# The begin of a kernel: 20 products of zeros, first loads in three pieces, token rows ahead of w1, statistics and the centring of w1 reordered

## The chip, the cores and the metric

The kernel runs on one core of a Trainium2 chip. The metric is device time in microseconds (us). Before the change the median of three runs is 933.14 us (932.35 to 933.66). One more execution was recorded by the hardware profiler; it took 934.63 us, and every start time below counts from the first instruction of that record.

A core has five engines that run side by side, each through its own list of instructions in order, and wait for each other by semaphores: TensorE (PE: matrix products, with its weight loads shown as PEld), VectorE (DVE), ScalarE (ACT), GpSimd (POOL) and SyncE (SP, which here only issues transfers). Transfers are issued by SP and ACT and carried by 16 shared DMA engines.

## The reference, cut to what matters

For S = 2048 tokens of D = 448 channels the kernel computes two branches of the same input x and mixes them by a gate:

```python
g = sigmoid((x * gate_w).sum(-1, keepdims=True))
a = attention(x, wq, wk, wv, wo)        # 16 heads of 28, one shared k and v
h = gelu(layernorm(x) @ w1)
hs = shifted(h) @ w2                    # four channel groups shifted by +1, -1, +2, -2 tokens
x1 = x + hs
b = x1 + gelu(layernorm(x1) @ w3) @ w4
return g * a + (1 - g) * b
```

The change is in the front part: the projection x @ wq (q, with k, v and the gate packed into spare columns) and the preparation of layernorm(x) @ w1.

## The kernel before, in words

**Number format.** Products that must be accurate are done as three products of split operands. A raw 32-bit tile is copied into a rounded "high" tile (`ah`, `wqh`, `w1h`; ACT) and the rest is kept in a "low" tile (`al`, `wql`, `w1l`; DVE). High by high, high by low and low by high are then summed in PSUM (`proj`, L132 to L139). The functions `split_x`, `split_w_chunk`, `split_w_high` and `split_w_low` do the splitting.

**Tiles.** xT holds x transposed, channels on partitions, in four chunks (c = 0 to 3) of 128 channels, the last one half full and held twice. Tokens are taken in four blocks b of 512. wq is laid out in the same four chunks; its 512 columns are four groups g of 128.

**Order.** The order of each engine's instructions is the order in which they stand in the program; nothing is rescheduled. Eight completion counters for transfers are handed round in program order, so that a transfer waits until the earlier transfer with its counter has landed.

**The front part, in order.**
- DVE clears `warm`, and PE multiplies it by itself 16 times (L97), products of zeros into `warm_ps` that nobody reads.
- ACT issues four transfers, one for each chunk of wq (L284), and SP four, one for each chunk of x of block 0 (L285), 256 KB each. Then ACT loads its table for Gelu (L286).
- `load_x(1)` brings x of block 1 (1 MB), then w1 (0.9 MB, L474). `load_x(2)` reuses the buffer of `wqraw`, and so waits for the last split of wq. Behind it come the token rows of blocks 0 and 1 (`load_x1`, 0.9 MB each, tile `x1`), w2 and the token rows of block 2.
- `first_queries` makes q of block 0 for the four groups. Chunk 0 is taken in full 32-bit products straight from the raw tiles (L316), since it has landed before anything is split; one such instruction is done as two passes, so that four instructions show as eight records. Chunks 1 to 3 follow as split products (L320).
- `stage_q(u)` for u = 4 to 11 makes q of blocks 1 and 2, 11 products each; ACT copies the result into one of four `qf` buffers (L308) and issues its write to memory (L309).
- For the layer norm before w1, only the factor 1/sqrt(var + eps) is applied after the product: `ln1_tile(b, t)` takes mean and variance of 128 tokens (DVE, L143 and L144; after the fourth, POOL raises to the power -0.5, L147 and L148), `ln1_send(b)` transposes the four columns on PE into the one-bank PSUM tile "misc" (L369), has ACT copy them (L371) and SP write them out, `ln1_read(b)` reads them back on every partition (`rsb`). The mean is taken off the weights instead: `sum_w1` adds the chunks of w1 on POOL (L385 to L387), `centre_w1` adds over partitions by a product with ones on PE, also into "misc" (L391), and takes the mean off each column on DVE (L393). `split_w_high` and `split_w_low` then split the centred w1.
- `stage_w1(0)` is the first stage that reads w1 (products `h`, L135 to L139); its results are scaled by `rsb` (L445).

In the program before, `sum_w1` stands behind the copies of `first_queries`, the statistics of block 0 behind `stage_q(5)`, `centre_w1` behind `stage_q(6)`, the sending of the statistics behind `stage_q(8)`, and the statistics of block 1 between `split_w_high` and `split_w_low`. The rest of the kernel (w2, w3 and w4, then attention with its exponentials) is not touched.

Of the kernel before, what the change touches and what calls it, by code (L numbers as in the profile page):

```python
# [10 lines left out]
F32R = mybir.dt.float32r  # L11
AF = mybir.ActivationFunctionType
# [4 lines left out]
P = 128  # L17
S = 2048
D = 448
# [17 lines left out]
def f32(ap):  # L37
    return ap.bitcast(F32)
# [3 lines left out]
def gated_mix_kernel(  # L42
# [12 lines left out]
    nc = tc.nc  # L55
# [18 lines left out]
    first = keep.tile([P, 4], F32, name="first")  # L74
    epst = keep.tile([P, 4], F32, name="epst")
    powt = keep.tile([P, 4], F32, name="powt")
# [12 lines left out]
    def misc_tile(name):  # L89
        return psA.tile([P, 512], F32, tag="misc", bufs=1, name=name)  # L90
# [2 lines left out]
        return psA.tile([P, 512], F32, tag="mx", bufs=1, name=name)  # L93

    wps = misc_tile("warm_ps")
    for _ in range(16):
        nc.tensor.matmul(wps[:, 0:256], warm[:, 0:P], warm, start=True, stop=True)  # L97

    def split_w_chunk(raw, wh, wl, c, cols=slice(None)):
# [9 lines left out]
    def split_w_high(raw, wh, wl):  # L109
        nc.scalar.copy(wh[:, 0:3, :], raw[:, 0:3, :])  # L110
        nc.gpsimd.memset(f32(wh)[64:128, 3, :], 0.0)
        nc.scalar.copy(wh[0:64, 3, :], raw[0:64, 3, :])
        nc.scalar.copy(wl[64:128, 3, :], raw[64:128, 3, :])

    def split_w_low(raw, wh, wl):
        for c in range(3):
            nc.vector.tensor_tensor(wl[:, c, :], raw[:, c, :], f32(wh)[:, c, :], ALU.subtract)
        nc.vector.tensor_tensor(wl[0:64, 3, :], raw[0:64, 3, :], f32(wh)[0:64, 3, :], ALU.subtract)
# [22 lines left out]
    def stats_tile(pool, b, t, mv):  # L141
        st = pool.tile([P, 6], F32, tag="st", bufs=4, name=f"st_{pool.name}_{b}_{t}")
        nc.vector.bn_stats(st, x1[:, 4 * b + t, :])  # L143
        nc.vector.bn_aggr(mv[:, t, :], st)  # L144

    def stats_end(mv, rs):
        nc.gpsimd.tensor_tensor(rs, mv[:, :, 1], epst, ALU.add)  # L147
        nc.gpsimd.tensor_tensor(rs, rs, powt, ALU.pow)  # L148

    def stats_tiles(pool, b):  # L150
        return (pool.tile([P, 4, 2], F32, tag="mv", bufs=2, name=f"mv_{pool.name}_{b}"),
                pool.tile([P, 4], F32, tag="rs", bufs=2, name=f"rs_{pool.name}_{b}"))
# [99 lines left out]
    with tc.tile_pool(name="s1b", bufs=1) as s1b, \  # L252
# [13 lines left out]
        xraw, xact = {}, {}  # L266

        def load_x(b):
            if b == 1:
                xraw[b] = f32(s1b.tile([P, 4, 512], F32R, tag="w2x", bufs=1, name="xkv_1"))  # L270
            else:
                xraw[b] = s1.tile([P, 4, 512], F32, tag="raw", bufs=2, name=f"xkv_{b}")
            nc.sync.dma_start(xraw[b], xT[:, :, 512 * b:512 * b + 512])

        def load_x1(b):
            nc.sync.dma_start(x1[:, 4 * b:4 * b + 4, :],
                              x[512 * b:512 * b + 512, :].rearrange("(t p) d -> p t d", p=P))

        wqraw = s1.tile([P, 4, 512], F32, tag="raw", bufs=2, name="wqraw")
        wqh = s1.tile([P, 4, 512], F32R, name="wqh")  # L280
        wql = s1.tile([P, 4, 512], F32R, name="wql")
        xraw[0] = s1.tile([P, 4, 512], F32, tag="raw", bufs=2, name="xkv_0")
        for c in range(4):
            nc.scalar.dma_start(wqraw[:, c, :], wq[:, c, :])  # L284
            nc.sync.dma_start(xraw[0][:, c, :], xT[:, c, 0:512])  # L285
        nc.scalar.activation(first, powt, AF.Gelu_apprx_tanh)  # L286
        w1h = s1.tile([P, 4, D], F32R, name="w1h")
        w1l = s1.tile([P, 4, D], F32R, name="w1l")
        w2h = s1b.tile([P, 4, D], F32R, name="w2h")
        w2l = s1b.tile([P, 4, D], F32R, name="w2l")  # L290
        hh, hl, acts = {}, {}, {}

        def split_x(b, c0, c1, high=True):
            if b not in xact:
                xact[b] = (s1.tile([P, 4, 512], F32R, tag="ah", bufs=3, name=f"ahk_{b}"),
                           s1.tile([P, 3, 512], F32R, tag="al", bufs=3, name=f"alk_{b}"))
            split_a(xraw[b], *xact[b], c0, c1, high)
# [7 lines left out]
        def q_out(u, ps):  # L305
            b, g = divmod(u, NG)
            qf = s1.tile([P, 512], F32, tag="qf", bufs=4, name=f"qf_{u}")
            nc.scalar.copy(qf, ps)  # L308
            nc.scalar.dma_start(qd[g, :, 512 * b:512 * b + 512], qf)  # L309
# [13 lines left out]
        def stage_q(u, tile_of=mm1):  # L323
            b, g = divmod(u, NG)
            ps = tile_of(f"q_{u}")
            w = slice(g * P, (g + 1) * P)
            proj(ps, wqh[:, :, w], wql[:, :, w], *xact[b])
            q_out(u, ps)
# [31 lines left out]
        def ln1_tile(b, t):  # L360
            if t == 0:
                rs1_of[b] = stats_tiles(s1, b)
            stats_tile(s1, b, t, rs1_of[b][0])
            if t == 3:
                stats_end(*rs1_of[b])

        def ln1_send(b):
            ps = misc_tile(f"rsT_{b}")[0:4, 0:P]
            nc.tensor.transpose(ps, rs1_of.pop(b)[1], ident)  # L369
            rT = s1.tile([4, P], F32, tag="rT", bufs=2, name=f"rT_{b}")  # L370
            nc.scalar.copy(rT, ps)  # L371
            rb_of[b] = dram.tile([4, P], F32, tag="rsd", bufs=2, name=f"rsd_{b}")
            nc.sync.dma_start(rb_of[b], rT)

        def ln1_read(b):
            rd = rb_of[b]
            rb_of[b] = s1.tile([P, 512], F32, tag="rsb", bufs=2, name=f"rsb_{b}")
            nc.sync.dma_start(rb_of[b][0:C], rd.rearrange("(o t) p -> o (t p)", o=1).broadcast_to([C, 512]))
# [5 lines left out]
        def sum_w1():  # L384
            nc.gpsimd.tensor_tensor(wsum, w1raw[:, 0, :], w1raw[:, 1, :], ALU.add)  # L385
            nc.gpsimd.tensor_tensor(wsum, wsum, w1raw[:, 2, :], ALU.add)
            nc.gpsimd.tensor_tensor(wsum[0:64], wsum[0:64], w1raw[0:64, 3, :], ALU.add)  # L387

        def centre_w1():
            ps = misc_tile("wsum_ps")[:, 0:D]  # L390
            nc.tensor.matmul(ps, ones, wsum, start=True, stop=True)  # L391
            for c in range(4):
                nc.vector.scalar_tensor_tensor(w1raw[:, c, :], ps, -1.0 / D, w1raw[:, c, :],  # L393
                                               op0=ALU.mult, op1=ALU.add)
# [75 lines left out]
                    between(t)  # L470

        load_x(1)
        w1raw = f32(s1b.tile([P, 4, 516], F32R, tag="hl", bufs=2, name="w1raw"))[:, :, 0:D]
        nc.sync.dma_start(w1raw, w1)  # L474
        split_x(0, 1, 2)
        split_w_chunk(wqraw, wqh, wql, 1)
        split_x(0, 2, 3)
# [3 lines left out]
        split_w_chunk(wqraw, wqh, wql, 0)  # L481
        q0 = first_queries()
        load_x(2)
        load_x1(0)
        load_x1(1)
        w2raw = f32(s1b.tile([P, 4, 516], F32R, tag="hh", bufs=2, name="w2raw"))[:, :, 0:D]
        nc.sync.dma_start(w2raw[0:C, :, :], w2.rearrange("(q p) n -> p q n", p=C))
# [2 lines left out]
        split_x(1, 2, 4)  # L490
        for g in range(NG):
            q_out(g, q0[g])
        sum_w1()
        split_x(2, 0, 2)
        split_x(2, 2, 4)
        split_x(0, 0, 1)
        stage_q(4, hs_tile)
        stage_q(5, hs_tile)
        for t in range(4):
            ln1_tile(0, t)  # L500
        stage_q(6)
        centre_w1()
        stage_q(7)
        stage_q(8)
        ln1_send(0)
        ln1_read(0)
        split_w_high(w1raw, w1h, w1l)
        for t in range(4):
            ln1_tile(1, t)
        split_w_low(w1raw, w1h, w1l)  # L510
        stage_q(9)
        load_x(3)
        stage_q(10)
# [614 lines left out]
```

## Time and profile before

| quantity | value |
|---|---|
| median of three runs | 933.14 us (932.35 to 933.66) |
| the profiled execution, its own time | 934.63 us |
| span of its record, first to last instruction | 932.8 us |
| mean granted TensorE clock | 0.997 |
| PE busy | 917.5 us, 98% of the span |
| ACT, DVE, POOL busy | 637.5 us, 513.7 us, 80.8 us |
| DMA over the span | 47.34 MB, 51 GB/s in the mean |

How to read the rows: a row of the timeline has start, duration, engine, line, operation, output <- inputs, shapes, how many were merged (x), and in brackets the idle time before it and what ended that. ACTq and SPq rows are the issuing of a transfer, not its movement. Matmuls are pipelined and the ends in the record are modelled: the distance between two starts is what a product costs in a stream. The load of the next product's weights (PEld) begins when the present product starts.

### The profile page before, as it was taken

To read this page: it belongs to the slowest core of one execution; us is meant where nothing else is said; L and a number is where in the kernel's file an instruction comes from. 1 tells how busy PE (TensorE), PEld (TensorE's weight loads), DVE (VectorE), ACT (ScalarE), POOL (GpSimd) and SP (SyncE) were. 2 spreads that over 40 slices of the span, in tenths; PEclk is the share of its full clock that TensorE was granted. 3 is DMA by queue.
4 is the path that set the end of the run, shared out by engine and by line. 5 is a ranking of instruction groups with operands and counts; after the bars stand their busy time and mean duration, and the time that the engine had idled before them with its cause. 6 is when DMAs were issued, how large, how long until landed. Compare 5 with 4: busy or idle time off the path is not lost.

```text
span 932.8 us, 24155 instructions
## 1 busy us (share of the span) xinstructions
PE 917.5 (98%) x10309; PEld 627.6 (67%) x10309; DVE 513.7 (55%) x940; ACT 637.5 (68%) x1006; POOL 80.8 (9%) x111
## 2 busy tenths in 40 slices
PE   9999999999999999999999999999999999999996
PEld 6788888888888888865555555555555555555553
DVE  3665274631431531156666676676667666766663
ACT  5542345331231231279999999999999999999994
POOL 3243320200000520020000000000000000000000
PEclk9999999999999999999999999999999999999998
DMA  9822643120210110020000001000011000010001
GB/s 305 291 75 55 179 139 116 39 65 1 50 37 1 40 46 0 1 61 14 24 15 24 13 30 49 20 18 15 24 43 34 15 24 13 26 52 7 11 14 44
DMA packets 40441, 47.34 MB, mean 51 GB/s; under 512 B 10120, under 2 KB 28488, under 8 KB 40328
## 3 DMA queue, kind: packets, MB, share of 16 engines
q1 hardware_dynamic: 37304, 40.27, 14.6%
q10 hardware_dynamic: 3024, 5.47, 1.7%
q8 instruction: 82, 1.34, 0.6%
q14 instruction: 31, 0.25, 0.1%
HBM read 32.56 MB, written 11.67 MB: 47 GB/s over the span
## 4 chain that ended last, share of the span: by engine, by line
PE 92%; ACT 4%; DMA 2%; issue 1%; DVE 1%; SPq 0%; ACTq 0%; DVEq 0%
PE bank L870 24%; PE bank L204 17%; PE acc L685 5%; PE bank L822 5%; PE acc L687 5%; PE acc L686 5%; PE g L135 4%; PE g L136 4%; PE g L137 4%; ACT p L859 4%; PE pair L204 2%; PE hs L463 1%; PE hs L464 1%; PE g L138 1%; PE g L139 1%; PE h L135 1%
## 5 line engine op out<-in xcount | busy, mean ns | idle before, releaser
L859 ACT ACTIVATE p<-bank 128x512 f32<-128x512 f32 x512 | 265.1, 608 | 16.3 <-PE pair L204 8.3
L870 PE MATMUL bank<-p,vext 128*32 128x256 f32 x3808 | 248.8, 397 | 5.7 <-ACT p L859 1.6
L870 PEld LDWEIGHTS bank<-p,vext 128*32 128x32 f32 x3808 | 110.7, 109 | 125.5 <-ACT p L859 59.7
L912 DVE COPY p<-pair 128x1024 f32<-128x1024 f32 x127 | 155.6, 1225 | 56.1 <-PE pair L204 47.5
L675 ACT ACTIVATE gh<-g 128x512 fp32r<-128x512 f32 x55 | 32.9, 598 | 185.3 <-PE g L139 185.3
L796 DVE TENSOR_TENSOR o<-o,bank 128x256 f32<-128x256 f32 (+1 forms) x206 | 91.0, 442 | 96.0 <-PE bank L870 81.7
L859 ACT ACTIVATE p<-p 128x1024 f32<-128x1024 f32 x127 | 139.3, 1097 | 0.0
L859 ACT ACTIVATE p<-pair 128x1024 f32<-128x1024 f32 x129 | 136.9, 1061 | 0.0
L677 DVE TENSOR_TENSOR gl<-gf,gh 128x512 fp32r<-128x512 f32 x55 | 38.3, 696 | 166.7 <-ACT gf L676 166.7
L204 PE MATMUL bank<-qh,kh 32*128 32x512 f32 x512 | 117.1, 447 | 0.0
L204 PE MATMUL pair<-qh,kh 32*128 32x512 f32 x512 | 116.3, 450 | 0.3 <-DVE x L742 0.3
L204 PE MATMUL bank<-ql,kh 32*128 32x512 f32 x512 | 103.5, 390 | 0.0
L204 PE MATMUL bank<-qh,kl 32*128 32x512 f32 x512 | 103.3, 388 | 0.0
L204 PE MATMUL pair<-qh,kl 32*128 32x512 f32 x512 | 101.3, 389 | 0.0
L204 PE MATMUL pair<-ql,kh 32*128 32x512 f32 x512 | 101.1, 389 | 0.0
L204 PEld LDWEIGHTS bank<-qh,kh 32*128 32x128 f32 x512 | 50.9, 182 | 57.5 <-issue 30.1
L685 PE MATMUL acc<-w4h,gh 128*128 128x448 f32 x220 | 80.5, 366 | 0.0
L687 PE MATMUL acc<-w4h,gl 128*128 128x448 f32 x220 | 80.1, 364 | 0.0
L686 PE MATMUL acc<-w4l,gh 128*128 128x448 f32 x220 | 80.0, 363 | 0.0
L135 PE MATMUL g<-ah,w3h 128*128 128x512 f32 x168 | 65.8, 392 | 0.0
L136 PE MATMUL g<-al,w3h 128*128 128x512 f32 x168 | 65.7, 391 | 0.0
L137 PE MATMUL g<-ah,w3l 128*128 128x512 f32 x168 | 65.7, 391 | 0.0
(206 smaller groups left out, 1415.8 us busy)
## 6 DMA issues: line engine op xcount, KB each, us to landing
qd<-qf ACTq DMA_DIRECT2D x16, 256.0 KB
rb<-rd SPq DMA_DIRECT2D x15, 256.0 KB
x<-in_x_dram SPq DMA_DIRECT2D x4, 896.0 KB
xd<-xt SPq DMA_DIRECT2D x16, 224.0 KB
w34raw<-in_w_dram SPq DMA_DIRECT2D x7, 512.0 KB
qr<-qd SPq DMA_DIRECT2D x64, 56.0 KB
out_dram<-ot SPq DMA_DIRECT2D x15, 224.0 KB
w34raw<-in_w_dram SPq DMA_DIRECT2D x7, 448.0 KB
```

What stands on the lines that cost most here:

```text
L135: nc.tensor.matmul(ps, wh[:, c, :], ah[:, c, :], start=(c == 0), stop=False)
L136: nc.tensor.matmul(ps, wh[:, c, :], al[:, c, :], start=False, stop=False)
L137: nc.tensor.matmul(ps, wl[:, c, :], ah[:, c, :], start=False, stop=False)
L204: nc.tensor.matmul(ps[j], k[h, keys], q[h, :], start=(r == 0), stop=(r == 2), tile_position=(32 * j, 0))
L685: nc.tensor.matmul(ps, gh[:, tok], w4h[i][:, k, :], start=(f == 0), stop=False)
L686: nc.tensor.matmul(ps, gh[:, tok], w4l[i][:, k, :], start=False, stop=False)
L687: nc.tensor.matmul(ps, gl[:, tok], w4h[i][:, k, :], start=False, stop=(f == stop))
L796: nc.vector.tensor_add(o, o, pv)
L822: nc.tensor.matmul(ps[32 * i:32 * i + 32, :], a[:, c:c + 32], w, start=True, stop=True, tile_position=(0, 32 * i))
L859: nc.scalar.activation(p[:, heads], p[:, heads] if source is None else source, AF.Exp, scale=SCALE)
L870: nc.tensor.matmul(pv[32 * j:32 * j + 32, :], vext[:, kt, :], p_of[k][:, j, qs], start=(k == ks[0]), stop=(k == ks[-1]), tile_position=(0, ...
L912: nc.vector.tensor_copy(pa[:, both], pairs[0])
```

## The change

1. 20 products of zeros instead of 16.
2. The first chunks of wq and x come in pieces: ACT issues the first 128 columns of wq (the group g = 0) and the upper 64 partitions of x, SP the lower 64 partitions of x and the other 384 columns of wq. Then chunks 1 to 3 as before, but ACT's table load now stands behind chunk 1 and ahead of chunks 2 and 3.
3. The token rows of block 0 are loaded right behind x of block 1, in the place that w1 had; w1 is loaded behind x of block 2.
4. The statistics of block 0 move up ahead of `sum_w1` (and so ahead of the splits of x of block 2), the sending and reading back of them from behind `stage_q(8)` to behind `stage_q(6)`, `centre_w1` from behind `stage_q(6)` to behind `stage_q(8)`, and `split_w_low` of w1 ahead of the statistics of block 1.

```diff
-    for _ in range(16):
+    for _ in range(20):
         nc.tensor.matmul(wps[:, 0:256], warm[:, 0:P], warm, start=True, stop=True)
...
-        for c in range(4):
+        nc.scalar.dma_start(wqraw[:, 0, 0:P], wq[:, 0, 0:P])
+        nc.sync.dma_start(xraw[0][0:64, 0, :], xT[0:64, 0, 0:512])
+        nc.scalar.dma_start(xraw[0][64:128, 0, :], xT[64:128, 0, 0:512])
+        nc.sync.dma_start(wqraw[:, 0, P:512], wq[:, 0, P:512])
+        for c in range(1, 4):
             nc.scalar.dma_start(wqraw[:, c, :], wq[:, c, :])
             nc.sync.dma_start(xraw[0][:, c, :], xT[:, c, 0:512])
-        nc.scalar.activation(first, powt, AF.Gelu_apprx_tanh)
+            if c == 1:
+                nc.scalar.activation(first, powt, AF.Gelu_apprx_tanh)
...
         load_x(1)
-        w1raw = f32(s1b.tile([P, 4, 516], F32R, tag="hl", bufs=2, name="w1raw"))[:, :, 0:D]
-        nc.sync.dma_start(w1raw, w1)
+        load_x1(0)
...
         load_x(2)
-        load_x1(0)
+        w1raw = f32(s1b.tile([P, 4, 516], F32R, tag="hl", bufs=2, name="w1raw"))[:, :, 0:D]
+        nc.sync.dma_start(w1raw, w1)
         load_x1(1)
...
+        for t in range(4):
+            ln1_tile(0, t)
         sum_w1()
         split_x(2, 0, 2)
         split_x(2, 2, 4)
         split_x(0, 0, 1)
         stage_q(4, hs_tile)
         stage_q(5, hs_tile)
-        for t in range(4):
-            ln1_tile(0, t)
         stage_q(6)
-        centre_w1()
+        ln1_send(0)
+        ln1_read(0)
         stage_q(7)
         stage_q(8)
-        ln1_send(0)
-        ln1_read(0)
+        centre_w1()
         split_w_high(w1raw, w1h, w1l)
+        split_w_low(w1raw, w1h, w1l)
         for t in range(4):
             ln1_tile(1, t)
-        split_w_low(w1raw, w1h, w1l)
```

## The prediction

> **What bounds the kernel now.** I read the page first, then the list of waits, then the timeline of the first 40 us. From the page: busy shares, PE over the span in 40 slices, and the chain that ended last.
>
> ```profile
> PE 917.5 (98%) x10309; PEld 627.6 (67%) x10309; DVE 513.7 (55%) x940; ACT 637.5 (68%) x1006; POOL 80.8 (9%) x111
> PE   9999999999999999999999999999999999999996
> PE 92%; ACT 4%; DMA 2%; issue 1%; DVE 1%; SPq 0%; ACTq 0%; DVEq 0%
> ```
>
> All that PE waited for, over the whole span (total, times, longest, in us):
>
> ```profile
> PE bank L870 <- ACT p L859: 1.6, 6, 0.3
> PE warm_ps L97 <- DVE warm L65: 1.0, 1, 1.0
> PE q L316 <- DMA wqraw<-in_wq_dram: 0.8, 1, 0.8
> PE pair L204 <- DVE x L742: 0.3, 1, 0.3
> ```
>
> and one of SP's own waits, used below:
>
> ```profile
> SPq L276 <- DMA x<-in_x_dram: 9.0, 1, 9.0
> ```
>
> TensorE bounds the kernel. Between its first useful product and attention it waits for nothing, so what the begin wins or loses on PE arrives undiminished at the end, unless a new wait takes it. An engine other than PE matters only where PE would wait for it. Now the begin, in the timeline:
>
> ```profile
> 0.72 1.86 ACTq L284 DMA_DIRECT2D wqraw<-in_wq_dram  x4
> 1.04 3.60 PE L97 MATMUL warm_ps<-warm 128*128 128x256 bf16 x16 [1.04 <-DVE warm L65]
> 2.62 1.28 ACT L286 ACT_TABLE_LOAD   x1 [2.62 <-issue]
> 5.41 5.94 PE L316 MATMUL q<-xkv,wqraw 128*128 128x512 f32 x8 [0.77 <-DMA wqraw<-in_wq_dram]
> ```
>
> and the weight loads of that stretch alone, one after the other:
>
> ```profile
> 6.42 0.34 PEld L316 LDWEIGHTS q<-xkv,wqraw 128*128 128x128 f32 x1 [0.52 <-issue]
> 7.28 0.34 PEld L316 LDWEIGHTS q<-xkv,wqraw 128*128 128x128 f32 x1 [0.52 <-issue]
> 8.13 0.34 PEld L316 LDWEIGHTS q<-xkv,wqraw 128*128 128x128 f32 x1 [0.52 <-issue]
> 8.98 0.34 PEld L316 LDWEIGHTS q<-xkv,wqraw 128*128 128x128 f32 x1 [0.52 <-issue]
> 9.84 0.25 PEld L316 LDWEIGHTS q<-xkv,wqraw 128*128 128x128 f32 x1 [0.52 <-issue]
> 10.32 0.19 PEld L316 LDWEIGHTS q<-xkv,wqraw 128*128 128x128 f32 x1 [0.24 <-issue]
> 10.76 0.19 PEld L320 LDWEIGHTS q<-ahk,wqh 128*128 128x128 f32 x1 [0.24 <-issue]
> 11.19 0.19 PEld L320 LDWEIGHTS q<-ahk,wqh 128*128 128x128 f32 x1 [0.24 <-issue]
> ```
>
> The zeros run from 1.04 to 4.64, then PE stands 0.77 us for the first load, and useful products begin at 5.41. Each load of weights marks the start of a product: 0.85 apart up to 9.84, then 0.48, 0.44, 0.43. PE's rate doubles at 9.84. The eight records of L316 took 11.19 - 5.41 = 5.78 us (the load at 11.19 marks the product behind them); at 0.43 they take 3.44. So **2.3 us** are lost here to a slow clock (the distances between starts show it).
>
> **The change part by part.** Durations are of the profiled execution: 934.63 us, its span 932.8 and 1.8 around it; that is 1.49 above the median of 933.14, to which I carry the difference.
>
> *20 zeros.* Four more cost at most 4 x 3.60/16 = 0.9 us, 4.64 to 5.54 by the ends in the record, which overlap the next start, so the first useful product is free to begin at about 5.4: they fill the pause and cost nothing while the data comes no earlier than now. If it came at 4.6, they would cost up to 0.9.
>
> *Pieces.* The first product now needs 64 KB of wq and both halves of x, 320 KB instead of 512 KB, in three transfers instead of two. No row has such a small first load; bounds are the end of the old zeros, 4.64, and, if a third transfer only adds its 0.4 us of issue, 5.8. I take 5.4, nearest to the row at 5.41, so this part is worth 0. [...]
>
> *Clock.* 3.60 us of zeros did not raise the rate, 5.41 to 9.84 = 4.43 us without a pause did. If it takes one unbroken run of a length between these, the unbroken run from 1.04 raises it between 4.64 and 5.47, and all but 0.06 us of the useful products run fast: -2.3. If the pause never mattered, 0. I take -2.3, as both rows speak for an unbroken run.
>
> *Loads and their queues.* The rows on which the rest hangs, picked from the timeline up to 40 us (most rows between them are left out):
>
> ```profile
> 8.47 0.62 ACT L101 CAST wqh<-wqraw 128x512 fp32r<-128x512 f32 x1
> 11.51 0.69 DVE L102 TENSOR_TENSOR wql<-wqraw,wqh 128x512 fp32r<-128x512 f32 x1 [0.26 <-ACT wqh L101]
> 12.27 0.54 SPq L273 DMA_DIRECT2D xkv<-in_xT_dram  x1
> 15.42 1.53 POOL L385 TENSOR_TENSOR wsum<-w1raw 128x448 f32<-128x448 f32 x1 [10.44 <-DMA w1raw<-in_w_dram]
> 18.58 1.15 POOL L387 TENSOR_TENSOR wsum<-wsum,w1raw 64x448 f32<-64x448 f32 x1
> 18.62 0.34 ACTq L309 DMA_DIRECT2D qd<-qf  x1
> 23.05 1.83 DVE L129 TENSOR_TENSOR alk<-xkv,ahk 128x1024 fp32r<-128x1024 f32 x2 [5.56 <-ACT ahk L126]
> 24.64 0.38 SPq L276 DMA_DIRECT2D x<-in_x_dram  x1
> 25.71 0.59 ACT L308 COPY qf<-q 128x512 f32<-128x512 f32 x1 [1.22 <-DMA qd<-qf]
> 25.97 0.91 PE L391 MATMUL wsum_ps<-wsum,ones 128*128 128x448 f32 x2
> 26.24 0.62 DVE L143 BATCH_NORM_STATS2 st_s<-x 128x6 f32<-128x448 f32 x1
> 26.90 0.18 DVE L144 BATCH_NORM_AGGREGATE mv_s<-st_s 128x2 f32<-128x6 f32 x1
> 28.79 0.59 ACT L308 COPY qf<-q 128x512 f32<-128x512 f32 x1 [0.45 <-DMA qd<-qf]
> 29.18 2.21 DVE L393 SCALAR_TENSOR_TENSOR w1raw<-wsum_ps,w1raw 128x448 f32<-128x448 f32 x4
> 31.75 0.27 PE L369 MATMUL rsT<-ident,rs_s 128*4 128x128 f32 x1
> 33.51 0.26 ACT L371 COPY rT<-rsT 4x128 f32<-4x128 f32 x1 [0.40 <-ACT qf L308]
> 33.67 1.31 ACT L110 CAST w1h<-w1raw 128x1344 fp32r<-128x1344 f32 x1
> 35.02 1.70 DVE L117 TENSOR_TENSOR w1l<-w1raw,w1h 128x448 fp32r<-128x448 f32 x3 [0.69 <-ACT w1h L110]
> 39.39 0.39 PE L135 MATMUL h<-ahk,w1h 128*112 128x512 f32 x1
> ```
>
> w1 was the second large load on SP and landed by 15.4; the token rows of block 0 were the fourth, and the transfer that waits for them goes out at 24.64. The two change places; no row shows w1 there, and the ends are 15.4 (its present landing) and, were it late, the last rival's. In the fourth place w1 lands at about 24.6; POOL needs 15.42 to 19.73 = 4.3 us for `sum_w1`, so the sum is ready at **28.9**.
>
> *Statistics of block 0 on DVE* (four times 0.8 us) move into the 5.56 us in which DVE idled before 23.05; their data now lands by 15.4. Without that cover the splits of x of block 2 end 3 us later, first read by `stage_q(8)`. Their POOL part comes ahead of `sum_w1` and is done before w1 lands. Cost 0. The sending goes to SP past nothing but loads already issued: 0.
>
> *centre_w1* (0.91 on PE, paid either way) now follows `stage_q(8)`. PE got to that point at 31.75 with the product already behind it; without it and 2.3 earlier it arrives at 31.75 - 0.91 - 2.3 = **28.5**. There it waits, with `stage_q(9)` queued behind, for two things. First the sum at 28.9. Second the one-bank tile: `rsT` now uses it before, and its copy `rT` stands on ACT behind the copy of `stage_q(6)`, which began at 28.79 because a buffer's write had not landed. If that write does not move, `rT` ends at 28.79 + 0.59 + 0.34 + 0.26 = 30.0, a wait of 1.5; if it moves with PE, at 27.7, none. These writes stood behind a backlog on SP (18.62 issued, buffer free at 25.71) that the change does not shorten, so I stay off the lower end: ready at 29.0, a wait of **0.5**.
>
> *Behind it* the chain to `h` is 0.91 + 2.21 on DVE + 1.31 on ACT and a first low part of 1.70/3 = 0.6, 5.0 us, against 39.39 - 31.75 = 7.6 us of products: hidden. The statistics of block 1, now behind w1's low split on DVE, are sent only inside `stage_w1(0)`, behind its third group of products: 0.
>
> Sum: 0 - 2.3 + 0.5 = **-1.8 us**: 932.8 for an execution like the profiled one, and 931.3 against the median. The bound of what a measurement can tell, 0.2%, is 1.87 us, so this lies on its edge.
>
> **The rivals.**
>
> *The clock is granted in fixed stretches.* If a whole stretch must be busy, its length lies between (9.84 - 5.41)/2 = 2.2 (a shorter one would have fitted earlier) and 4.43. Without the pause the rate rises one stretch earlier, which saves half its length, 1.1 to 2.2, in the middle 1.65; PE then comes to the sum at 29.2 and hardly waits: 931.6. [...]
>
> *rT is as late as 30.0*: wait 1.5, gain 0.8, 932.3. For it speaks the backlog; against it that each write is issued 2 us sooner.
>
> *The change doesn't do what it says*: the pause stays, since the data is later than 5.6, or doesn't matter: gain 0, 933.1. Against it the two runs above.
>
> *Slower: the last chunks of wq come late.* ACT issued all four chunks within 0.72 to 2.58. Now chunks 2 and 3 stand behind the 1.28 us table load, and their counters are those of the second half of x and the rest of chunk 0: they go out after about 5.2 and 5.7, when SP has put 1.9 MB in front. A transfer so placed took 7.1 us (18.62 to 25.71); then chunk 2 lands at 12.3. Behind it stand five splits on ACT (0.62 each, as at 8.47), the last of which is chunk 0's, and the one on DVE (0.69) that `load_x(2)` waits for: it ends at 16.1 instead of 12.20, and w1 moves by the 3.9. The sum is ready at 32.8, and `stage_q(9)` starts at 33.7 instead of 31.8: 1.9 later, 935.0. It decides from a lateness of 1.9 (28.9 + 1.9 + 0.91 = 31.7: no gain left). Against it: wq was not held up before, and a transfer at the start took some 4.7 us (0.72 to 5.41), with which chunk 2 lands at 9.9 and little moves.
>
> **How the numbers follow.** Forecast 931.3 (own range 930.6 to 931.9): 0.38, of which 0.20 beyond 0.2%. No wait at all, or an execution that was slow longer before, down to 929.8: 0.16. Fixed stretches 931.6: 0.17 (0.07 beyond). rT late: 0.10. No effect: 0.06. Late wq: 0.13, of which 0.09 slower by more than 0.2% and 0.04 within it. Faster 0.20 + 0.16 + 0.07 = 0.43, slower 0.09, the same 0.48. The range 929.9 to 933.3 leaves out most of the slower case and the tip of the fastest.
>
> **What would show it.** Zeros to 5.5 with no pause of 0.5 before L316; distances of 0.43 from about 5.5 (or 6.5 by stretches); a wait of PE at the product with ones below 1 us; `sum_w1` from 24.6. Wrong if L316 starts after 5.8, if the rate rises after 7.6, if `load_x(2)` is issued after 14, or if PE waits more than 1 us at L396.

## The result and the profile after

The kernel became slower, not faster: 937.93 us in the median (936.54 to 939.25, 7 runs) against 933.14 (932.15 to 934.80, 7 runs) before, a ratio of 1.0046 [1.0035, 1.0056] (ratios here are those of the recorded comparison; the two medians alone give 1.0051). The forecast was 931.3, its range 929.9 to 933.3. The profiled execution took 936.58 us with a span of 934.8, so the two records (934.63 before) lie 2.0 us apart, the medians 4.8: the record of before was one of its slower executions, that of after one of its faster.

The first reading answers the first of before: busy time by engine, and the chain that ended last, from the page of the kernel after.

```profile
PE 916.4 (98%) x10313; PEld 626.8 (67%) x10313; DVE 513.0 (55%) x940; ACT 637.0 (68%) x1006; POOL 80.5 (9%) x111
PE 90%; ACT 5%; DMA 3%; issue 1%; DVE 1%; SPq 0%; ACTq 0%; DVEq 0%
```

TensorE has no more work than before (916.4 against 917.5), yet the span is longer, so it waits. What for, in the list of PE's waits of the kernel after (total, times, longest):

```profile
PE wsum_ps L396 <- ACT rT L376: 2.7, 1, 2.7
PE q L325 <- ACT wqh L101: 1.5, 1, 1.5
PE bank L875 <- ACT p L864: 1.4, 5, 0.3
PE warm_ps L97 <- DVE warm L65: 1.0, 1, 1.0
PE pair L204 <- DVE x L747: 0.3, 1, 0.3
```

The first two are new; the 0.8 for the first load of wq is gone. Their places are in the timeline of the kernel after, here its first 17 us (rows between are left out):

```profile
1.04 3.79 PE L97 MATMUL warm_ps<-warm 128*128 128x256 bf16 x20 [1.04 <-DVE warm L65]
...
2.38 1.28 ACT L291 ACT_TABLE_LOAD   x1 [2.38 <-issue]
...
3.46 0.63 SPq L273 DMA_DIRECT2D xkv<-in_xT_dram  x1
4.07 1.72 ACTq L288 DMA_DIRECT2D wqraw<-in_wq_dram  x2
...
4.67 3.65 PE L321 MATMUL q<-xkv,wqraw 128*128 128x512 f32 x8
...
11.92 0.62 ACT L101 CAST wqh<-wqraw 128x512 fp32r<-128x512 f32 x1 [3.46 <-DMA wqraw<-in_wq_dram]
...
12.59 1.19 PE L325 MATMUL q<-ahk,wqh 128*128 128x512 f32 x4 [1.50 <-ACT wqh L101]
...
15.92 0.56 SPq L273 DMA_DIRECT2D xkv<-in_xT_dram  x1
```

The zeros run into the first useful product without a pause, at 4.67. But ACT's issue of chunks 2 and 3 of wq (4.07, two of them) stands behind SP's issue of x of block 1 (3.46). Chunk 2 is split only at 11.92, and PE has waited 1.5 us for it; and with the splits late, the buffer of `wqraw` comes free late and `load_x(2)` goes out at 15.92 instead of 12.27. In the meantime the DMA engines run dry. Stretches of the kernel after, the last two columns being the DMA's busy share and GB/s:

```profile
14.00:15.00 1.00, 1.00 (x6) 0.79 (x5) 0.68 (x1) 0.97 (x2) 0.00 (x0) 1.00 0.21 79
15.00:16.00 1.00, 1.00 (x6) 0.83 (x5) 0.69 (x1) 1.00 (x3) 0.00 (x0) 1.00 0.02 9
```

w1 stands in the same queue behind `load_x(2)`. The rows around the product with ones, from ACT's, POOL's and PE's timelines of the kernel after:

```profile
25.54 0.58 ACT L313 COPY qf<-q 128x512 f32<-128x512 f32 x1
28.07 0.33 ACTq L314 DMA_DIRECT2D qd<-qf  x1
...
29.53 0.59 ACT L313 COPY qf<-q 128x512 f32<-128x512 f32 x1 [0.46 <-DMA qd<-qf]
32.06 0.33 ACTq L314 DMA_DIRECT2D qd<-qf  x1
32.43 0.26 ACT L376 COPY rT<-rsT 4x128 f32<-4x128 f32 x1 [2.31 <-DMA x<-in_x_dram]
```

```profile
28.06 1.14 POOL L390 TENSOR_TENSOR wsum<-w1raw 128x448 f32<-128x448 f32 x1 [4.85 <-DMA w1raw<-in_w_dram]
...
30.50 1.12 POOL L392 TENSOR_TENSOR wsum<-wsum,w1raw 64x448 f32<-64x448 f32 x1
```

```profile
32.83 0.99 PE L396 MATMUL wsum_ps<-wsum,ones 128*128 128x448 f32 x2 [2.69 <-ACT rT L376]
```

w1 lands at 28.06 and its sum is ready at 31.62; the copy `rT`, which frees the shared bank, is later still, at 32.69. It stands on ACT behind writes of `qf` that go out only when a load has landed (28.07 with w1, 32.06 with rows of x): ACT's copy of 25.54 ends at 26.1, and its write waits 2 us, ACT with it. From here to attention nothing new is lost: PE reaches the first product of `h` at 41.19 instead of 39.39,

```profile
41.19 0.39 PE L135 MATMUL h<-ahk,w1h 128*112 128x512 f32 x1
```

and attention's first scores at 405.76 instead of 403.95, both 1.8 later.

### The profile page after: what moved, and what is told of

Same layout as the page of the kernel before. It is cut to its first block, busy times and chain, and to the rows that moved or that the text cites. A ratio compares the mean times of both kernels' runs of the same rounds, so it can differ in the third digit from the quotient of the medians.

```text
span 934.8 us, 24170 instructions
## 1 busy us (share of the span) xinstructions
PE 916.4 (98%) x10313; PEld 626.8 (67%) x10313; DVE 513.0 (55%) x940; ACT 637.0 (68%) x1006; POOL 80.5 (9%) x111
## 4 chain that ended last, share of the span: by engine, by line
PE 90%; ACT 5%; DMA 3%; issue 1%; DVE 1%; SPq 0%; ACTq 0%; DVEq 0%
PE bank L875 25%; PE bank L204 17%; PE bank L827 5%; PE acc L690 5%; PE acc L692 5%; PE acc L691 5%; ACT p L864 4%; PE g L135 4%; PE g L136 4%; PE g L137 4%; PE pair L204 2%; DMA x<-in_x_dram 2%; PE hs L468 1%; PE hs L469 1%; PE g L138 1%; PE g L139 1%
```

## The experiments

Three theories. A: the first loads as they are now (the first chunks in pieces, and the table load between chunks 1 and 2) make chunks 2 and 3 of wq late, and the rest shifts. B: the new order of statistics and centring costs by itself. C: the wait at the product with ones is that of the bank it shares with `rsT`. This table has all results; ratios are to the kernel before, timed beside each. "h" is the start of the first product of `h`, "scores" that of attention's first product into `pair`, each in the one record of that kernel (us).

| kernel | median, us | ratio | h | scores |
|---|---|---|---|---|
| before, first record | 933.14 | | 39.39 | 403.95 |
| before, second record (e8) | 933.08, one run | | 37.77 | 402.25 |
| the change | 937.93 | 1.0046 [1.0035, 1.0056] | 41.19 | 405.76 |
| e1: zeros alone | 932.81 | 0.9995 [0.9986, 1.0004] | 37.83 | 402.42 |
| e2: pieces and table alone | 936.19 | 1.0028 [1.0018, 1.0039] | 40.89 | 405.44 |
| e3: zeros, pieces and table | 936.41 | 1.0029 [1.0018, 1.0041] | 40.43 | 404.96 |
| e4: zeros and order | 933.09 | 0.9999 [0.9989, 1.0008] | 37.05 | 401.61 |
| e5: change, chunks 2, 3 on SP | 933.64 | 1.0003 [0.9994, 1.0012] | 38.30 | 402.85 |
| e6: change, table last | 933.60 | 1.0003 [0.9994, 1.0011] | 38.88 | 403.46 |
| e7: change, `rsT` in its own bank | 935.40 | 1.0024 [1.0014, 1.0034] | 39.48 | 403.95 |
| e9: zeros, table moved, no pieces | 938.23 | 1.0055 [1.0042, 1.0068] | 42.21 | 406.77 |
| e10: change with milder loads | 932.79 | 0.9998 [0.9989, 1.0006] | 36.99 | 401.55 |

**e1, zeros alone**

```diff
-    for _ in range(16):
+    for _ in range(20):
```

> The kernel before with 20 products of zeros instead of 16, nothing else. Theory A (late wq: the two added transfers push wq's chunks 2 and 3, and with them x of block 2 and w1, back) and theory B (reordering: w1 in the fourth place and the one-bank tile make PE wait) both expect a gain, as the pause before the first useful product closes: the products of L316 at 0.43 from the start or soon after it, 1.0 to 2.3 us less, cut by a wait of at most 1.2 us at L369, because the factors of the layer norm are ready at 30.7. Theory C (the zeros themselves cost) expects 0.5 us more or no change.

The timeline of e1:

```profile
1.04 4.00 PE L97 MATMUL warm_ps<-warm 128*128 128x256 bf16 x20 [1.04 <-DVE warm L65]
5.40 3.70 PE L316 MATMUL q<-xkv,wqraw 128*128 128x512 f32 x8 [0.36 <-DMA wqraw<-in_wq_dram]
```

The eight records take 3.70 us and the first `h` comes 1.56 earlier than in the first record of before. In the times, however, only 0.77 us are left (932.81 against 933.58 beside it), and the interval holds 1. The gain of 1.0 to 2.3 that both theories expected is missed. The lowest times are alike (931.87 and 931.78); what the zeros cut is the top: 12 of the 26 executions of before lie above e1's highest, 933.72.

**e8, the kernel before once more**

> The kernel before, one more execution with its records. If the clock's rise comes at a place that changes from execution to execution, the first eight records of useful products can take anything from 3.4 to 5.8 us, and the loss of 2.3 us that the prediction read is that of one execution; if the rise is fixed by the pause before the first useful product, they take about 5.8 again, with starts 0.85 apart up to about 9.8.

In the first record of before the eight weight loads of L316 took about 0.34 us each until 9.84, as the prediction shows. In the second record, e8 (nanoseconds least, median, most; first and last start in us):

```profile
L316 PEld LDWEIGHTS q<-xkv,wqraw x8: 186/190/191, 5.4 to 8.1; 128*128 128x128 f32 x8
```

The same program, with the same pause (0.78 us here, 0.77 there), has all eight at the full rate this time (last start 8.1 instead of 10.3), and is 1.7 us earlier at attention. So the place where the clock rises changes from execution to execution, and the 2.3 us belong to some executions of before only. The two records also show that a pause of 0.8 us does not always prevent the rise. In e8 `h` starts at 37.77, as early as in e1 (37.83): against an execution whose clock rose early, the zeros win nothing.

**e2 and e3, pieces and table without the new order**

```diff
+        nc.scalar.dma_start(wqraw[:, 0, 0:P], wq[:, 0, 0:P])
...
-        nc.scalar.activation(first, powt, AF.Gelu_apprx_tanh)
+            if c == 1:
+                nc.scalar.activation(first, powt, AF.Gelu_apprx_tanh)
```

(the whole of part 2 of the change, of which these are two places; e3 has the 20 zeros as well)

> The kernel before with the first loads in pieces and the table load moved, 16 zeros, old order. Theory A expects chunk 2 of wq to land at about 12 instead of 8.5, a wait of PE at the split products of 1 to 3 us, load_x(2) issued at about 16 instead of 12.3, and a time 1 to 4 us above before. Theory B expects no more than 0.5 us of difference.

> 20 zeros and the pieces, old order of loads and statistics. Theory A: as the run with pieces alone, less the clock's gain: 0 to 3 us above before. Theory B: 1 to 3 us below before.

The timeline of e3:

```profile
12.07 0.62 ACT L101 CAST wqh<-wqraw 128x512 fp32r<-128x512 f32 x1 [2.92 <-DMA wqraw<-in_wq_dram]
...
16.05 0.54 SPq L273 DMA_DIRECT2D xkv<-in_xT_dram  x1
```

Chunk 2 at 12.07 and `load_x(2)` at 16.05, as in the change: against e1, `h` is 2.60 later. e2, with 16 zeros, splits chunk 2 at 11.96. Both times lie where theory A had them, 2.6 and 2.8 us above the kernel before beside them. The loss is in part 2.

**e4, zeros and order without pieces** (the change with the first loads of before, table behind them)

```diff
-        nc.scalar.dma_start(wqraw[:, 0, 0:P], wq[:, 0, 0:P])
...
+        for c in range(4):
             nc.scalar.dma_start(wqraw[:, c, :], wq[:, c, :])
             nc.sync.dma_start(xraw[0][:, c, :], xT[:, c, 0:512])
+        nc.scalar.activation(first, powt, AF.Gelu_apprx_tanh)
```

> The changed kernel without the pieces: 20 zeros, and loads, statistics and centring in the new order. Theory A: load_x(2) back at 12.3, w1 lands by 25, the wait of PE at the product with ones falls from 2.7 to below 1 us, and the time lies 1 to 2.3 us below before. Theory B: the wait stays at 1.5 us or more and the time is at or above that of before.

The timeline of e4:

```profile
24.06 1.16 POOL L385 TENSOR_TENSOR wsum<-w1raw 128x448 f32<-128x448 f32 x1 [3.16 <-DMA w1raw<-in_w_dram]
...
28.33 0.25 ACT L371 COPY rT<-rsT 4x128 f32<-4x128 f32 x1 [0.40 <-ACT qf L308]
...
28.74 0.98 PE L391 MATMUL wsum_ps<-wsum,ones 128*128 128x448 f32 x2
```

B falls: PE does not wait at the product with ones, and `h` starts 0.78 earlier than in e1. A's time, 1 to 2.3 us below before, did not come either: the interval of the ratio holds 1. Against e3 the same order makes `h` 0.76 *later*: in these records it costs only where w1 is already late. The 0.78 do not reach the end: from the first scores to the last product attention takes 521.9 us here, 520.7 in e1.

**e9, the table's place alone** (first loads whole, 20 zeros)

```diff
         for c in range(4):
             nc.scalar.dma_start(wqraw[:, c, :], wq[:, c, :])
             nc.sync.dma_start(xraw[0][:, c, :], xT[:, c, 0:512])
-        nc.scalar.activation(first, powt, AF.Gelu_apprx_tanh)
+            if c == 1:
+                nc.scalar.activation(first, powt, AF.Gelu_apprx_tanh)
```

> The kernel before with 20 zeros and with ScalarE's table load put between its issues of chunk 1 and chunk 2 of wq, all first loads whole. What of the pieces' loss is due to the table's place alone? If it takes the small first pieces as well (with whole loads the next x is still issued near 5.4, when the first chunk of wq has landed, so that chunk 2, issued near 4, stays ahead of it): attention starts within 0.7 us of the kernel with 20 zeros alone (402.4), time 932.3 to 933.8. If the table's place does it alone: chunk 2 of wq splits after 11 us, attention starts at 404 to 405.5, time 935 to 936.5.

The timeline of e9:

```profile
1.65 1.28 ACT L287 ACT_TABLE_LOAD   x1 [1.65 <-PEq L1117]
...
2.58 0.73 SPq L273 DMA_DIRECT2D xkv<-in_xT_dram  x1
...
3.36 0.71 SPq L475 DMA_DIRECT2D w1raw<-in_w_dram  x1
...
5.59 0.82 ACTq L284 DMA_DIRECT2D wqraw<-in_wq_dram  x2
...
12.68 0.62 ACT L101 CAST wqh<-wqraw 128x512 fp32r<-128x512 f32 x1 [4.41 <-DMA wqraw<-in_wq_dram]
```

The second answer holds, beyond its own numbers: one line moved, no piece anywhere, and the kernel is as slow as the whole change, or slower (1.0055 against 1.0046, intervals that overlap). The table is done at 2.9, but ACT issues chunk 2 only at 5.59. The records of the transfers say what each waits for, here in order of issue with the counter that each raises:

```
e9   ACT 0.72 chunk 0    counter 100     SP 0.72 x chunk 0     counter 102
     ACT 1.16 chunk 1    counter 104     SP 1.18 to 2.11       counters 105, 106, 107
     SP  2.58 load_x(1)  counter 108     SP 3.36 w1            counter 109
     ACT 5.59 chunk 2    counter 100, waits for chunk 0 of wq
     ACT 5.96 chunk 3    counter 102, waits for chunk 0 of x
```

The eight counters were not handed round in the order of the program text, as the description of the kernel has it: chunk 2 stands ahead of `load_x(1)` and w1 in the text, yet these two took the last free counters, and chunk 2 had to wait for one of the first to come free. With the table load behind all four chunks it is `load_x(1)` that waits (issued at 5.38 in e1, at 2.58 in e9). In the change it went the same way: chunk 2 waited for the counter of x's upper half and chunk 3 for that of the rest of chunk 0, as the prediction had read it; these pieces landed sooner, and chunk 2 went out at 4.07.

**e5 and e6, the change with part 2 mended in two ways**

```diff
-            nc.scalar.dma_start(wqraw[:, c, :], wq[:, c, :])
+            (nc.scalar if c == 1 else nc.sync).dma_start(wqraw[:, c, :], wq[:, c, :])
```

> The changed kernel whole, but chunks 2 and 3 of wq are issued by SyncE's queue, ahead of the x rows that follow them, and no longer by ScalarE's behind them. Theory A (chunks 2 and 3 of wq come late because they stand behind x of the same tokens and behind the 1 MB of the next x, and everything behind them in the raw buffers shifts): the first split of chunk 2 starts at 8 to 9.5 us and not at 11.9, the second next x is issued at 12 to 13.5 and not at 15.9, the wait of TensorE at the product with ones falls from 2.7 to under 1 us, attention starts about 2.5 to 4 us earlier than 405.8, and the time is 932 to 934. Rival (small first transfers cost by their number, whatever queue and order): chunk 2 stays at 11.5 to 12, time 936 to 938.

```diff
-            if c == 1:
-                nc.scalar.activation(first, powt, AF.Gelu_apprx_tanh)
+        nc.scalar.activation(first, powt, AF.Gelu_apprx_tanh)
```

> The changed kernel whole, but the load of ScalarE's function table stands behind its issues of all four chunks of wq and no longer behind the first two. Chunk 2 is then issued before the table's 1.28 us, near 2.4 and not 4.07. Theory A in the form that the issue time decides: chunk 2 gets ahead of the 1 MB of the next x, its first split starts at 8 to 9.5, the second next x is issued at 12 to 13.5, time 932 to 934. Rival A2 (what delays the chunks is the split of x by tokens alone, or the number of transfers, not when ScalarE issues): chunk 2 stays near 12, time 936 to 938.

Both bring the time back to that of the kernel before, at 1.0003, and PE's wait at the product with ones is gone in both. That part of A holds. PE's waits in e6:

```profile
PE bank L874 <- ACT p L863: 1.3, 5, 0.3
PE q L324 <- ACT wqh L101: 1.1, 1, 1.1
PE warm_ps L97 <- DVE warm L65: 1.0, 1, 1.0
PE pair L204 <- DVE x L746: 0.3, 1, 0.3
```

The times of the loads were missed: chunk 2 is split at 10.47 in e5 and 11.27 in e6, `load_x(2)` goes out at 14.51 and 15.10. What comes late here is already chunk 1, split at 9.34 and 9.90 instead of 7.33 in the change; PE waits 1.6 and 1.1 us for it. Stretches of e5 (last column GB/s),

```profile
5.00:6.00 1.00, 1.00 (x3) 0.30 (x2) 0.00 (x0) 0.00 (x0) 0.00 (x0) 1.00 1.03 230
6.00:7.00 1.00, 1.00 (x4) 0.44 (x3) 0.00 (x0) 0.00 (x0) 0.00 (x0) 1.00 0.98 270
```

and the same two of the kernel before, its second record:

```profile
5.00:6.00 1.00, 0.58 (x2) 0.34 (x3) 0.00 (x0) 0.00 (x0) 0.00 (x0) 1.00 1.06 404
6.00:7.00 1.00, 1.00 (x4) 0.52 (x3) 0.00 (x0) 0.30 (x1) 0.00 (x0) 1.00 1.05 404
```

With the pieces the engines are as busy in e5 but move 43% and 33% less just then. The other records with these pieces (the change, e2, e3, e6, e7) move less too, by amounts that differ: 239 to 328 GB/s in the first of these stretches and 256 to 373 in the second, against 399 and 408 in the first record of before and 404 in both in the second, where the first loads are whole. e6 differs from e4 in the pieces alone, and its `h` is 1.83 later: that is their own price in these two records. In the times (1.0003 against 0.9999) it is not clear of noise. Why the rate falls isn't settled.

**e7, the change with `rsT` in a bank of its own**

```diff
-            ps = misc_tile(f"rsT_{b}")[0:4, 0:P]
+            ps = max_tile(f"rsT_{b}")[0:4, 0:P]
```

> The changed kernel whole, but the transposed statistics lie in a PSUM bank of their own and not in the one they share, so that the transposition and its copy have nothing of the misc tile to wait for. Theory C (the wait of 2.7 us at the product with ones is the bank's: the copy to rT waits behind the q copy and write of block 6): wait falls to about 1.5, where the sum of w1 (31.6) takes over, time 1.2 lower, 936 to 937. Theory A: the copy to rT is held by ScalarE's own order behind a write that waits for loads, and the bank is beside the point: wait stays 2.7, time as the changed kernel, 937 to 938.

PE's waits and timeline of e7:

```profile
PE wsum_ps L396 <- POOL wsum L392: 0.9, 1, 0.9
```

```profile
31.13 1.02 PE L396 MATMUL wsum_ps<-wsum,ones 128*128 128x448 f32 x2 [0.94 <-POOL wsum L392]
```

C holds for its part: `rT` is copied as late as in the change (at 32.35), PE no longer cares and waits only for w1's sum. `h` is 1.71 earlier than in the change, and the ratio falls from 1.0046 to 1.0024, about that of e3 (1.0029). The expectation had 1.2 us, from an unchanged landing of w1, which was 0.6 earlier here. The late chunks remain, and the kernel is still slower than before.

**e10, milder first loads** (the change with these)

```diff
+        nc.scalar.dma_start(wqraw[:, 0, 0:P], wq[:, 0, 0:P])
+        nc.sync.dma_start(xraw[0][:, 0, :], xT[:, 0, 0:512])
+        nc.scalar.dma_start(wqraw[:, 0, P:512], wq[:, 0, P:512])
+        for c in range(1, 4):
+            nc.sync.dma_start(xraw[0][:, c, :], xT[:, c, 0:512])
+            nc.scalar.dma_start(wqraw[:, c, :], wq[:, c, :])
+        nc.scalar.activation(first, powt, AF.Gelu_apprx_tanh)
```

> The changed kernel with milder first loads: only the first chunk of wq is in two pieces (the 128 columns of the first product, then the rest), both on ScalarE's queue; the first chunk of x is whole and SyncE carries x alone; the table load stands behind the chunks of wq. Zeros and the new order as in the changed kernel. If the cause is what the theory says (chunks 2 and 3 overtaken by the next x, and a transfer rate that the many small first pieces lower between 4 and 7 us), both are gone: first product at 4.6 to 5.0, chunk 2 split by 9.5, no wait at the product with ones, attention starts at 401 to 402, and the time is 932 to 933, below both kernels, though hardly by more than 0.1% against the kernel before. Rival (any split of the first chunk lowers the rate, or what comes in attention eats the gain): attention from 402.3 on, or time 933.2 to 934.5.

The timeline of e10:

```profile
5.08 3.91 PE L319 MATMUL q<-xkv,wqraw 128*128 128x512 f32 x8
...
8.90 0.63 ACT L101 CAST wqh<-wqraw 128x512 fp32r<-128x512 f32 x1 [0.32 <-DMA wqraw<-in_wq_dram]
```

The front part is the shortest of all records (`h` at 36.99) and has no wait at the product with ones, though the first product came at 5.08, not by 5.0; the zeros run up to it. Attention then takes 521.9 us, as in e4, and the time is 0.9998 [0.9989, 1.0006] of the kernel before. The 932 to 933 are met (932.79), "below both kernels" is not: the kernel before took 932.53 beside it. What comes in attention eats the gain, as the rival had it. No version here beats it by more than can be measured.

## Why the prediction was wrong

*Zeros, cost 0*: right for the change. They fill the pause, and PE goes over into useful products without a gap:

```profile
L321 PEld LDWEIGHTS q<-xkv,wqraw x8: 186/190/192, 4.6 to 7.3; 128*128 128x128 f32 x8
```

(the weight loads of the first useful products in the kernel after, columns as for e8). In e1 and e4 0.4 us of the pause stayed, as the last zeros ran fast and ended early (the 20 took 4.00 and 3.88 us); in e3 and e6, whose zeros all ran slow (4.45 us), they held the first product to 5.28, while it came at 4.43 in e2 with 16.

*Pieces, worth 0, first product at 5.4*: the step that failed. The first product came at 4.67, at the lower end; but the part as a whole cost 2.6 us at `h` (e3 against e1), because of the line that the sum did not price, the table load between chunks 1 and 2. Alone, without any piece, it costs 4.38 at `h` (e9 against e1); with it behind all chunks the change is back at 1.0003 (e6). The term looked at the first product and not at the chunks of wq behind it. The prediction did have the mechanism, as its slower rival, and its places were close: chunk 2 at 12.3 (11.92), `load_x(2)` at 16.1 (15.92), the sum of w1 at 32.8 (31.62), `stage_q(9)` at 33.7 (33.31). The prediction gave this rival 0.13, on the ground that "a transfer at the start took some 4.7 us". That row was of a transfer with nothing large ahead of it; behind SP's 1 MB it took 11.92 - 4.07 = 7.9. The row it had for a transfer behind a backlog, 7.1, was the nearer one. The rival's 935.0 is 936.5 for an execution like the profiled one, and the profiled one of after took 936.58; the median of after is 1.4 higher than that. That it came so near is in part luck: w1's sum was 1.2 earlier than the rival had it, and `rT`, which it did not price, came 1.1 behind the sum. Of the four signs of being wrong that the prediction named, two came: `load_x(2)` after 14 and more than 1 us of wait at L396.

What the halves of x are worth by themselves no run separates. With halves the first product came straight behind the zeros, as early as 4.43 (e2), so its data was there by then; in e10, with x whole, the zeros run up to it at 5.08, which does not tell; and the transfer rate is lower behind the halves (230 to 328 GB/s between 5 and 6 us), but in e10 too (318).

*Clock, -2.3*: the eight loads of L321 in the record of after are all at the full rate, the last at 7.3, but neither the rule nor the size was right. The rise did not come from an unbroken run of 3.60 to 4.43 us. In the change the loads of the zeros already fall from 151 to 98 ns, by the single records from 4.0 on, which is 3.0 us after the first zero:

```profile
L97 PEld LDWEIGHTS <-warm x20: 98/151/151, 1.0 to 4.5; 128*128 128x128 bf16 x20
```

In e3 PE runs without a pause from 1.04 too, and its loads turn fast only after more than 5 us:

```profile
6.13 0.34 PEld L321 LDWEIGHTS q<-xkv,wqraw 128*128 128x128 f32 x1 [0.52 <-issue]
6.81 0.19 PEld L321 LDWEIGHTS q<-xkv,wqraw 128*128 128x128 f32 x1 [0.34 <-issue]
```

The prediction's rival at 0.17 rested on fixed stretches of the clock; no run shows such stretches or a length of them, only that the place of the rise differs (the last section has the places). In the change it lay before the first useful product; in e3 and e6, with the same 20 zeros, it lay behind it. The low end of the range, 929.8, counted on an execution that was slow for longer before: of these records the first one of before has the latest rise. As for the size: the profiled execution of before lay 1.49 above its median, and part of that was this very loss; e8 has none of it. The term, carried to the median, should have been near the 0.8 of e1.

*w1 at 24.6, its sum at 28.9, rT at 29.0, PE there at 28.5*: right for the begin that was assumed; e4 has 24.06, 28.34, 28.58 and 28.74, and no wait where 0.5 was forecast. In the change all moved with the late chunks: 28.06, 31.62, 32.69, PE at 30.14, and a wait of 2.7. That it is 2.7 and not the 1.5 up to the sum at 31.62 is the shared bank's doing (e7), which the prediction named but bounded at 30.0.

*Statistics on DVE, the sending, the chain behind the product, cost 0*: nothing in the records of e4 or of the change speaks against it; PE has no wait at `h`. No run tests them singly.

The sum in the runs' own terms, by starts of `h` in one record each: 37.83 with the zeros, + 2.60 for pieces and table, + 0.76 for the order on top of them = 41.19, the change's own.

Still open: why attention takes 520.7 to 521.9 us in these records though nothing in it was changed. PE's waits differ by place from record to record: at a product of the output projection (L822) the list of e8 has 0.5 us in one wait and that of e4 0.2, that of e1 none. In the records of e4 and e10 the longer attention ate the front part's gain. No run separates the cause.

## What to carry to other kernels

An instruction put between issues of transfers can reorder more than its own engine: here it changed which transfer had to wait for a completion counter, and 512 KB that were needed first were issued (at 5.59 in e9) behind 1 MB that was needed later (at 2.58). Read from the lists which transfer waits for which counter, and price a transfer by a row that had the same backlog ahead of it. Before a loss seen in one record is booked as gain, see how far that execution lies above the median: what it has more than the others can't be won in all of them.

## What the runs showed of the hardware

In e9 two queues did not share the DMA engines evenly: two chunks were issued on ACT's queue (q10) from 5.59 on; between 7 and 9 us all packets were still those of SP's queue (q1), which had been given 1.9 MB earlier (packets, MB and share of the 16 engines in that window):

```profile
q1 hardware_dynamic: 379, 0.74, 102.1%
```

From 9.5 to 12 both moved:

```profile
q1 hardware_dynamic: 300, 0.55, 57.8%
q10 hardware_dynamic: 237, 0.44, 47.1%
```

From 7 to 9 no packet of ACT's queue moved, though 256 KB twice had been issued there. So chunk 2 was late for two reasons: none of its packets moved between 1.4 and 3.4 us after its issue (in the first record of before chunk 0, issued at 0.72, had its first packet 1.2 us later), and then it shared the engines. What held it for so long is open.

The rise of the clock has no fixed place: in the first record of before the loads of weights turn fast at 9.84, in the second all eight of L316 are fast, from 5.4. With 20 zeros they turn fast at 4.0 in the change, and between 6.13 and 6.81 in e3. Two traces also give the time from which the full clock was granted: 9.95 in the first record of before and 4.02 in the change, within 0.11 us of the loads. By these starts PE had run without a pause for 3.0 us in the change, for at least 5.1 in e3 and for 4.4 in the first record of before; in e8 the first load behind the pause of 0.78 us, at 5.42, is already fast. No single length of unbroken run fits these four. What places the rise they don't show.
